# Attention keys cut into three chunks of 128 and one shared tail chunk; scores of batches 1 to 3 as stacked products

## The chip, the cores and the metric

The kernel runs on one core of one Trainium2 chip. The profile names the engines PE (TensorE, the matrix engine), PEld (its loading of weights), DVE (VectorE), ACT (ScalarE), POOL (GpSimd) and SP (SyncE, which issues most DMAs). The metric is the device time of one execution in microseconds; several executions are timed and their median is given. One more execution is profiled.

## What is computed

Softcapped attention over 4 batches, 12 heads, 448 positions and head width 64, and behind it two feed-forward layers over all 1792 positions, all in float32:

```python
scores = (q @ k^T) / sqrt(64)
scores = cap * tanh(scores / cap)
attn = softmax(scores)
x = attn @ v                      # heads side by side: 1792 x 768
x = relu(x @ w_in)**2 @ w_out     # 768 -> 2048 -> 768
h = x @ w2_in
out = (h * sigmoid(1.702 * h)) @ w2_out
```

## The kernel before

**Precision.** Every float32 operand is split into a rounded part and a rest (hi and lo), both in the engine's fast float32 form, and a product is made of two or three such products that add up in PSUM: hi x hi, hi x lo, lo x hi. The split takes one instruction on ACT (the copy that rounds) and one on DVE (the subtraction).

**Attention, by pairs of heads.** The path that runs is `bounded_cap`; `any_cap` (lines 21 and on) stands behind a branch for large caps and isn't taken. There are 6 pairs in each of 4 batches. `load_pair` fetches Q and K of a pair so that head A takes partitions 0 to 63 and head B 64 to 127 once they are transposed (`transposed`: by PE in batch 0, by DVE in batches 1 to 3). `prep_k` and `prep_q` split them into `kk` and `qq`. The 448 keys are cut into 4 chunks of 112. For each chunk `scores` makes, for each head, three products with 64 rows of contraction (line 893): 6 products, the heads alternating between the upper and the lower 64 rows. The result has keys on 112 partitions and both heads' 448 queries behind each other, 896 columns. `tanhs` and `exps` go over it on ACT, `split_hi` (ACT, in batch 0 DVE for chunks 0 and 2) and `split_lo` (DVE) split it into `phi` and `plo`, and `pv` multiplies it with the split V: 4 products per chunk (line 961). The sums of the exponentials over the keys are made in batch 0 by PE, 4 products per chunk with a matrix that has one column of ones (`key_sum`, line 947); in batches 1 to 3 DVE first adds the four chunks (`add_keys`, line 928), and PE sums the total.

**Feed-forward.** Each batch has 68 units of work (`units`); `product` (line 1198) makes 18 or 15 full products of 128 x 128 x 448 in a unit, `ahead` prepares weights for later units (`rebias` and the `wh` of `split_w` on ACT, `join` and the `wl` of `split_w` on DVE), `finish` takes the results out. In the first batch the weights come in a packed 64-bit form and need `rebias` and `join`; the joined weights are kept in DRAM for the other batches.

**Order.** `PLAN` gives each step of a pair its place, `attn_sub` runs one step of time for all pairs under way, a pair begins every 8 steps, and the main loop at the end sets as many steps of the next batch's attention behind each unit as spread them over a batch's units. The framework's scheduler then orders each engine's queue by what it reckons can start, within the limits of the tiles' buffers: `hi` and `lo` have 3 each (pool `e_p`), `x32` has 7, the K and Q tiles have 2. Each engine works through its queue in order. POOL issues the stores of batches 0 to 2 and the constants' memsets; SP issues the loads.

Of the kernel before, what the change touches and what calls it, by code (L numbers as in the profile page):

```python
# [677 lines left out]
def bounded_cap(ctx, tc, q, k, v, cap, w1, w2, w3, w4, out):  # L678
# [14 lines left out]
    nc = tc.nc  # L693
# [6 lines left out]
    NCH = S // CP  # L700
# [5 lines left out]
    Q_V = nc.sync  # L706
    Q_OUT = nc.gpsimd
# [24 lines left out]
    X32B = 7  # L732
# [34 lines left out]

    spread = [const.tile([P, 2, D], F32R, name=f"spread{i}") for i in range(NP)]
    sums = const.tile([P, S], F32, name="sums")
    rcp = const.tile([P, 2, S], F32R, name="rcp")  # L770

    def emit_const():
# [11 lines left out]
        nc.gpsimd.memset(f32(one[:, P - 1 : P]), 1.0)  # L784
        nc.gpsimd.memset(f32(rcp), 0.0)
# [15 lines left out]

    def load_pair(b, p):
        if b in DVE_QK:

            qt = ld.tile([P, S // 32, 32], F32, tag="q", name="qt")
            kt = ld.tile([P, S // 32, 32], F32, tag="k", name="kt")
            for t, src in ((kt, k), (qt, q)):
                for j in range(4):
                    Q_LOAD.dma_start(
                        out=t[32 * j : 32 * j + 32],  # L810
                        in_=src[b, 2 * p + j // 2, :, 32 * (j % 2) : 32 * (j % 2) + 32].rearrange(
                            "(c p) d -> p c d", p=32
                        ),
                    )
        else:
            qt = ld.tile([CP, NCH, 2, D], F32, tag="q", name="qt")
            kt = ld.tile([CP, NCH, 2, D], F32, tag="k", name="kt")
            for t, src in ((kt, k), (qt, q)):
                for j in range(2):
                    Q_LOAD.dma_start(  # L820
                        out=t[:, :, j, :], in_=src[b, 2 * p + j].rearrange("(p c) d -> p c d", c=NCH)
                    )
        raw[b, p] = (qt, kt)

    def transposed(b, t, name):

        if b in DVE_QK:
            y = ld.tile([P, S], F32, tag="tt", name=name)
            nc.vector.transpose(y, t.rearrange("p c d -> p (c d)"))
            return y  # L830
        ps = ps_x.tile([P, 512], F32, tag="x", name=name)
        for c in range(NCH):
            cols = slice(c, S, NCH) if name == "qps" else slice(c * CP, (c + 1) * CP)
            nc.tensor.transpose(ps[:, cols], t[:, c].rearrange("p h d -> p (h d)"), ident[:CP, :CP])
        return ps[:, :S]

    def load_v(b, p):
        vt = v_p.tile([CP, NCH, 2, D], F32, tag="vraw", name="vraw")
        for j in range(2):
            src = v[b, 2 * p + j]  # L840
            Q_V.dma_start(
                out=vt[:, :, j, :],
                in_=src.rearrange("(c p) d -> p c d" if b in DVE_QK else "(p c) d -> p c d", c=NCH),
            )
        vst[b, p] = vt

    def split_v(b, p, half):

        if half == 0:
            t = vst[b, p]  # L850
            vs = v_p.tile([CP, NCH, 4, D], F32R, tag="v", name="vs")
            vst[b, p] = (t, vs)
            nc.scalar.activation(vs[:, :, 0::3, :], t, AF.Copy)
        else:
            t, vs = vst[b, p]
            nc.vector.tensor_tensor(vs[:, :, 1:3, :], t, f32(vs[:, :, 0::3, :]), ALU.subtract)
            vst[b, p] = vs

    def prep_k(b, p, step):
# [60 lines left out]
    def add_keys(b, p, c):  # L920
# [3 lines left out]
        if c == 1:  # L924
            acc[b, p] = e_p.tile([CP, 2, S], F32, tag="acc", name="acc", bufs=1)
            et[b, p, NCH] = acc[b, p]
        a = acc[b, p]
        nc.vector.tensor_tensor(a, et[b, p, 0] if c == 1 else a, et[b, p, c], ALU.add)

    def key_sum(b, p, c):  # L930
# [5 lines left out]
        last = (p == p1 - 1 or not whole) and (c == NCH - 1 or not whole)  # L936
# [6 lines left out]
        hi, lo = hl[b, p, c]  # L943
        for j in range(2):
# [423 lines left out]
```

## Time and profile before

| | us |
|---|---|
| median of 3 timed runs | 1208.27 (1207.53 to 1212.91) |
| profiled execution | 1207.45 |
| its span in the profile | 1205.6 |

| engine | busy us | share of the span | instructions |
|---|---|---|---|
| PE | 1179.2 | 98% | 5832 |
| PEld | 1019.6 | 85% | 5832 |
| DVE | 848.8 | 70% | 1173 |
| ACT | 783.1 | 65% | 1129 |
| POOL | 48.4 | 4% | 83 |

The chain that ended last, followed back from the last instruction, is PE for 88% of the span, ACT for 7% and DVE for 2%. Of the 5832 matrix instructions 4608 belong to the feed-forward, 576 to the scores, 384 to the value products. A row of the timeline gives the start of an instruction, or of several alike in a row, how long they lasted from the first start to the last end, and what they read and write; matrix instructions overlap, so their price is read from one start to the next.

### The profile page before, as it was taken

The numbers are of one execution on the slowest core, as the hardware profiler recorded it, in microseconds if no ns is written. First come the engines' busy times: TensorE is split into PE (matmuls) and PEld (weight loads), VectorE is DVE, ScalarE is ACT, GpSimd is POOL, SyncE is SP. The second block draws the span as 40 slices with busy tenths as digits, with TensorE's granted clock in tenths as the row PEclk, the third lists the DMA queues.
The fourth block names the chain that finished last, engine by engine and source line by source line (L and its number), as shares of the span: only waits on it lengthen the run. The fifth ranks groups of instructions, "written<-read, shape, count | busy, mean of one in ns | idle before, by whom it ended". The sixth has DMA issues, their size and how long they took to land.

```text
span 1205.6 us, 15747 instructions
## 1 busy us (share of the span) xinstructions
PE 1179.2 (98%) x5832; PEld 1019.6 (85%) x5832; DVE 848.8 (70%) x1173; ACT 783.1 (65%) x1129; POOL 48.4 (4%) x83
## 2 busy tenths in 40 slices
PE   6999999999999999999999999999999999999996
PEld 4667988888777888888888888888899999999996
DVE  5799778998899956777577965667646753565354
ACT  6997898999878756677666566566643444344431
POOL 1000000000000400000000310000000310000000
PEclk9999999999999999999999999999999999999999
DMA  7555988788877855334323532223223442333333
GB/s 177 133 125 149 345 257 248 214 244 236 255 224 209 247 144 114 100 110 118 100 81 105 141 110 92 78 89 105 79 92 99 145 131 92 113 111 108 101 106 49
DMA packets 193225, 174.06 MB, mean 144 GB/s; under 512 B 116466, under 2 KB 165618, under 8 KB 193138
## 3 DMA queue, kind: packets, MB, share of 16 engines
q1 hardware_dynamic: 185266, 168.13, 46.9%
q0 software_dynamic: 2304, 4.13, 1.7%
q10 hardware_dynamic: 5568, 0.69, 0.4%
q8 instruction: 48, 0.79, 0.3%
q14 instruction: 39, 0.32, 0.1%
HBM read 142.25 MB, written 30.67 MB: 143 GB/s over the span
## 4 chain that ended last, share of the span: by engine, by line
PE 88%; ACT 7%; DVE 2%; issue 1%; SPq 1%; DMA 1%; DVEq 0%; ACTq 0%
PE mps L1198 76%; PE sps L893 5%; PE vps L961 5%; ACT e L904 2%; PE sums L947 1%; ACT e L900 1%; ACT phi L914 1%; ACT ct L979 1%; ACT wh L1178 1%; PE rps L1034 1%; ACT sx L1154 1%; SPq L820 0%; DVE plo L918 0%; DVE wl L1179 0%; DVE y L1161 0%
## 5 line engine op out<-in xcount | busy, mean ns | idle before, releaser
L1198 PE MATMUL mps<-g,wh 128*128 128x448 f32 x1536 | 442.2, 368 | 1.5 <-ACT g L1227 0.8
L1198 PE MATMUL mps<-xt,wh 128*128 128x448 f32 x1536 | 440.9, 368 | 0.5 <-ACT wh L1178 0.4
L1178 ACT ACTIVATE wh<-wraw 128x768 fp32r<-128x768 f32 (+1 forms) x204 | 164.7, 808 | 277.8 <-PE mps L1198 264.8
L1198 PEld LDWEIGHTS mps<-g,wh 128*128 128x128 f32 x1536 | 285.7, 188 | 36.9 <-ACT wh L1178 4.9
L1198 PEld LDWEIGHTS mps<-xt,wh 128*128 128x128 f32 x1536 | 286.0, 188 | 33.9 <-issue 5.1
L1179 DVE TENSOR_TENSOR wl<-wraw,wh 128x768 fp32r<-128x768 f32 (+1 forms) x204 | 185.4, 909 | 174.6 <-ACT wh L1178 173.0
L1198 PE MATMUL mps<-g,wl 128*128 128x448 f32 x768 | 281.3, 366 | 1.0 <-DVE wl L1179 1.0
L1198 PE MATMUL mps<-xt,wl 128*128 128x448 f32 x768 | 281.1, 366 | 0.3
L1198 PEld LDWEIGHTS mps<-g,wl 128*128 128x128 f32 x768 | 144.2, 188 | 14.2 <-DVE wl L1179 1.9
L1198 PEld LDWEIGHTS mps<-xt,wl 128*128 128x128 f32 x768 | 144.3, 188 | 13.3 <-DVE wl L1179 1.0
L1227 ACT ACTIVATE g<-r 128x448 fp32r<-128x448 f32 x128 | 73.4, 574 | 66.9 <-DVE r L1223 33.5
L918 DVE TENSOR_TENSOR plo<-e,phi 112x896 fp32r<-112x896 f32 x96 | 103.7, 1081 | 13.6 <-ACT phi L914 13.1
L1228 DVE TENSOR_TENSOR g<-r,g 128x448 fp32r<-128x448 f32 x128 | 79.6, 622 | 47.2 <-ACT g L1227 46.8
L904 ACT ACTIVATE e<-e,ecap 112x896 f32<-112x896 f32 x96 | 99.7, 1041 | 1.3
L893 PE MATMUL sps<-qq,kk 64*112 64x448 f32 x576 | 92.5, 404 | 2.7 <-ACT qq L879 1.7
L1240 DVE SCALAR_TENSOR_TENSOR y<-mps,y 128x448 f32<-128x448 f32 x96 | 59.5, 620 | 49.2 <-PE mps L1198 48.5
L900 ACT ACTIVATE e<-sps 112x896 f32<-112x896 f32 x96 | 87.2, 911 | 6.1 <-PE sps L893 5.9
L1256 POOL DMA_DIRECT2D out_dram<-o x72 | 45.2, 635 | 927.8 <-DVE o L1254 927.0
L914 ACT ACTIVATE phi<-e 112x896 fp32r<-112x896 f32 x84 | 79.6, 947 | 3.0 <-PE vps L961 1.2
L893 PEld LDWEIGHTS sps<-qq,kk 64*112 64x112 f32 x576 | 45.9, 174 | 40.3 <-issue 18.7
L961 PE MATMUL vps<-plo,vs 112*128 112x448 f32 x192 | 69.6, 374 | 3.4 <-DVE plo L918 3.4
L1179 DVE TENSOR_TENSOR wl<-y,wh 128x768 fp32r<-128x768 f32 (+1 forms) x68 | 61.5, 904 | 14.7 <-ACT wh L1178 14.2
(69 smaller groups left out, 1033.5 us busy)
## 6 DMA issues: line engine op xcount, KB each, us to landing
wraw<-keep SPq DMA_DIRECT2D x66, 768.0 KB, 4.3
wraw<-in_moe_w_in_dram SPq DMA_DIRECT2D x32, 766.5 KB, 6.5
wraw<-keep SPq DMA_DIRECT2D x36, 640.0 KB, 4.4
keep<-y SPq DMA_DIRECT2D x44, 384.0 KB, 3.2
wraw<-in_moe_w_out_dram SPq DMA_DIRECT2D x24, 638.8 KB, 6.1
wraw<-in_moe_w_out_dram SPq DMA_DIRECT2D x12, 766.5 KB, 6.6
keep<-y SPq DMA_DIRECT2D x24, 320.0 KB, 3.2
vraw<-in_v_dram SPq DMA_DIRECT2D x48, 112.0 KB, 3.8
```

What stands on the lines that cost most here:

```text
L893: nc.tensor.matmul(ps[:CP, j, :S], kk[r, ik, c * CP : (c + 1) * CP], qq[r, iq, :], start=(i == 0), stop=(i == 2),)
L900: nc.scalar.activation(e, sc.pop((b, p, c))[:CP, :, :S], AF.Tanh)
L904: nc.scalar.activation(e, e, AF.Exp, scale=ecap[:CP])
L914: nc.scalar.activation(hi, e, AF.Copy)
L918: nc.vector.tensor_tensor(lo, et[b, p, c], f32(hi), ALU.subtract)
L961: nc.tensor.matmul(pvp[b, p][j][:, :S], a, t[:, j, :], start=(c == 0 and n == 0), stop=(c == NCH - 1 and n == 1),)
L1178: nc.scalar.activation(hi[:, :kn], t[:, :kn], AF.Copy)
L1179: nc.vector.tensor_tensor(lo[:, :kn], t[:, :kn], f32(hi[:, :kn]), ALU.subtract)
L1198: nc.tensor.matmul(ps[:, :S], a[:, kk, :], r, start=(kk == 0 and i == 0), stop=(kk == kn - 1 and i == 2),)
L1227: nc.scalar.activation(g[:, 0, :], r, AF.Copy)
L1228: nc.vector.tensor_tensor(g[:, 1, :], r, f32(g[:, 0, :]), ALU.subtract)
L1240: nc.vector.scalar_tensor_tensor(y, ps[:, :S], scale, y, ALU.mult, ALU.add)
```

## The change

The 448 keys of a head become three full chunks of 128 and a tail of 64. The K tile is 512 columns wide with zeros in it, so that the tail of head A stands in columns 64 to 127 on its partitions and the tail of head B in columns 0 to 63 on its own; one tail chunk of 128 rows serves both heads, and its scores are 448 columns wide, not 896. V is loaded to match: head A's full chunks are its keys 64 to 447, head B's its keys 0 to 383, and one more slot holds both tails.

In batches 1 to 3 (`STACKED`) the hi and lo parts of Q lie above each other on the 128 partitions, in one tile per head, and K's hi and lo parts are each copied to the other 64 partitions by a DMA on POOL's queue (`prep_k`, step 3). One product of 128 rows then makes K hi with Q hi and with Q lo at once, a second one K lo with both: two products per head and chunk, four per chunk, and four for the tail. The splits of K and Q are done in two instructions of 64 partitions each. In batch 0 the three full chunks keep their six products of 64 rows; the tail has three of 128 rows.

`pv` has four products for a full chunk and four of 64 rows for the tail. `hi` and `lo` get two buffers instead of three, `x32` six instead of seven.

The diff, cut to its core:

```diff
-    NCH = S // CP
+    NCH = 4
+    TAIL = NCH - 1
+    KW = NCH * P
+    STACKED = (1, 2, 3)
...
+    Q_DUP = nc.gpsimd
...
-    X32B = 7
+    X32B = 6
...
+    kz = [const.tile([P, KW], F32, name=f"kz{i}") for i in range(2)]
...
+    def emit_zeros():
+        for t in kz:
+            nc.gpsimd.memset(t, 0.0)
...
     def load_pair(b, p):
+        kt = kz[p % 2]
...
-            kt = ld.tile([CP, NCH, 2, D], F32, tag="k", name="kt")
...
+            Q_LOAD.dma_start(out=kt[16:, :, 0, :], in_=ka)
+            Q_LOAD.dma_start(out=kt[32:, :, 1, :], in_=kb[:96])
+            Q_LOAD.dma_start(out=kt[:16, :, 1, :], in_=kb[96:])
+            Q_LOAD.dma_start(out=qt[:, :, 0, :], in_=qa)
+            Q_LOAD.dma_start(out=qt[:, :, 1, :], in_=qb)
...
     def load_v(b, p):
...
+        vt = v_p.tile([P, 2 * TAIL + 1, D], F32, tag="vraw", name="vraw")
+        va, vb = v[b, 2 * p], v[b, 2 * p + 1]
+        Q_V.dma_start(out=vt[:, 0 : 2 * TAIL : 2, :], in_=va[64:].rearrange("(c p) d -> p c d", p=P))
+        Q_V.dma_start(out=vt[:, 1 : 2 * TAIL : 2, :], in_=vb[: TAIL * P].rearrange("(c p) d -> p c d", p=P))
+        Q_V.dma_start(out=vt[64:, 2 * TAIL, :], in_=va[:64])
+        Q_V.dma_start(out=vt[:64, 2 * TAIL, :], in_=vb[TAIL * P :])
...
     def prep_k(b, p, step):
...
+            if stacked:
+                for j, r, o in halves():
+                    nc.scalar.activation(kk[r, j, 0, :], ps[r], AF.Copy)
+            else:
+                nc.scalar.activation(kk[:, 0, :], ps, AF.Copy)
...
+        elif stacked:
+            kk = prep[b, p][1]
+            for j, r, o in halves():
+                Q_DUP.dma_start(out=f32(kk[o, j]), in_=f32(kk[r, j]))
...
     def scores(b, p, c):
...
-        for i, (ik, iq) in enumerate(((0, 0), (0, 1), (1, 0))):
-            for j in range(2):
-                r = slice(64 * j, 64 * j + 64)
-                nc.tensor.matmul(
-                    ps[:CP, j, :S], kk[r, ik, c * CP : (c + 1) * CP], qq[r, iq, :],
-                    start=(i == 0), stop=(i == 2),
-                )
+        tail = c == TAIL
+        cols = slice(0, P) if tail else slice((c + 1) * P, (c + 2) * P)
+        if b in STACKED:
+            todo = [(0 if tail else j, kk[:, j, i, cols], qq[:, j, :]) for j in range(2) for i in range(2)]
+        elif tail:
+            todo = [(0, kk[:, ik, cols], qq[:, iq, :]) for ik, iq in ((0, 0), (0, 1), (1, 0))]
...
+    def width(c):
+
+        return slice(0, 1 if c == TAIL else 2)
...
-        hi = e_p.tile([CP, 2, S], F32R, tag="hi", name="phi")
-        lo = e_p.tile([CP, 2, S], F32R, tag="lo", name="plo")
+        hi = e_p.tile([P, 2, S], F32R, tag="hi", name="phi", bufs=2)[:, width(c), :]
+        lo = e_p.tile([P, 2, S], F32R, tag="lo", name="plo", bufs=2)[:, width(c), :]
...
+        if c == TAIL:
+            for j, r, o in halves():
+                nc.vector.tensor_tensor(a[o, j, :], a[o, j, :], e[o, 0, :], ALU.add)
...
+        if c == TAIL:
+
+            todo = [(j, vt[o, 2 * TAIL], t[o, 0, :]) for t in hl[b, p, c] for j, r, o in halves()]
...
-        -5: [(prep_q, 0)],
+        -5: [(prep_q, 0), (prep_k, 3)],
```

**PE's order, at unit 34 of batch 0's feed-forward** (about 230 us in the trace of before). Units are counted from 0. Names: `mps` is a unit's product, `vps` a value product, `sps` scores, `sums` the key sums, each with its buffer number; `wh` and `wl` are split weights. Before, from the end of unit 33 to the start of unit 34:

```order
L1198 MATMUL mps_2443<-g_2210,wh_2378 128x448 x2
L1198 MATMUL mps_2443<-g_2210,wl_2379 128x448
L961 MATMUL vps_2244<-phi_2388,vs_2087 128x448
L961 MATMUL vps_2244<-plo_2389,vs_2087 128x448
L961 MATMUL vps_2245<-phi_2388,vs_2087 128x448
L961 MATMUL vps_2245<-plo_2389,vs_2087 128x448
L1198 MATMUL mps_2489<-xt_675,wh_2418 128x448 x2
L1198 MATMUL mps_2489<-xt_675,wl_2419 128x448
```

The changed kernel at the same place: the end of unit 33, the tail's four products, the next scores.

```order
L1282 MATMUL mps_2452<-g_2218,wh_2384 128x448 x2
L1282 MATMUL mps_2452<-g_2218,wl_2385 128x448
L1045 MATMUL vps_2252<-phi_2394,vs_2093 128x448
L1045 MATMUL vps_2253<-phi_2394,vs_2093 128x448
L1045 MATMUL vps_2252<-plo_2395,vs_2093 128x448
L1045 MATMUL vps_2253<-plo_2395,vs_2093 128x448
L967 MATMUL sps_2538<-qq_2209,kk_2055 128x448 x4
L1030 MATMUL sums_2578<-phi_2478,one_118 128x448
```

And after seven more products the end of that block and the start of unit 34:

```order
L1045 MATMUL vps_2584<-plo_2487,vs_2434 128x448
L967 MATMUL sps_2601<-qq_2209,kk_2055 128x448 x4
L1045 MATMUL vps_2584<-phi_2589,vs_2434 128x448
L967 MATMUL sps_2699<-qq_2543,kk_2399 128x448
L1045 MATMUL vps_2583<-plo_2590,vs_2434 128x448
L1045 MATMUL vps_2584<-plo_2590,vs_2434 128x448
L967 MATMUL sps_2699<-qq_2543,kk_2399 128x448 x3
L1045 MATMUL vps_2583<-phi_2645,vs_2434 128x448
L1045 MATMUL vps_2584<-phi_2645,vs_2434 128x448
L1282 MATMUL mps_2500<-xt_675,wh_2425 128x448 x2
```

Before, the four products of one chunk stand between units 33 and 34. Now 30 products stand there: the tail, the last scores and the sums of one pair, and the value products of two chunks and part of a third of the next pair.

**ACT's order at the same place.** `wh` 2378, 2418 and 2463 are the weights of units 33, 34 and 35; `e` is tanh (from `sps`) or exp, `phi` the rounding copy. Before:

```order
L1178 ACTIVATE wh_2378<-y32_2333 128x640
L1245 ACTIVATE xt_703<-y_1294 128x448
L900 ACTIVATE e_2391<-sps_2346 112x896
L904 ACTIVATE e_2391<-e_2391,ecap_113 112x896
L914 ACTIVATE phi_2477<-e_2391 112x896
L1245 ACTIVATE xt_913<-y_1294 128x448
L1178 ACTIVATE wh_2418<-y32_2374 128x768
L1154 ACTIVATE sx1_116<-wraw_2341 128x768
L900 ACTIVATE e_2480<-sps_2429 112x896
L1178 ACTIVATE wh_2463<-y32_2414 128x768
```

The changed kernel, where `wh_2384` (nine rows further up) are the weights of unit 33 and `wh_2425` those of unit 34:

```order
L982 ACTIVATE e_2489<-e_2489,ecap_113 128x896
L992 ACTIVATE phi_2486<-e_2397 128x896
L1329 ACTIVATE xt_1018<-y_1296 128x448
L1063 ACTIVATE ct_2530<-vps_2252 64x448
L1063 ACTIVATE ct_2530<-vps_2253 64x448
L992 ACTIVATE phi_2589<-e_2489 128x896
L978 ACTIVATE e_2592<-sps_2538 128x896
L982 ACTIVATE e_2592<-e_2592,ecap_113 128x896
L992 ACTIVATE phi_2645<-e_2592 128x896
L1262 ACTIVATE wh_2425<-y32_2380 128x768
L1238 ACTIVATE sx1_116<-wraw_2349 128x768
```

Before, five instructions stand between the weights of unit 33 and those of unit 34, one of them a `phi`. Now there are seventeen, and these are the last of them: three of the `phi` read or replace what the block on PE works on.

**SP's order at the start of the program** (its first loads; `kz` and `kt` are K tiles, `capt` the cap). Before:

```order
L820 DMA kt<-in_k_dram 112x4x64 x2
L820 DMA qt<-in_q_dram 112x4x64 x2
L773 DMA capt<-in_cap_dram 128x1
L820 DMA kt<-in_k_dram 112x4x64 x2
L820 DMA qt<-in_q_dram 112x4x64 x2
L841 DMA vraw<-in_v_dram 112x4x64 x3
```

The changed kernel, from the same place; three more rows for the first pair's V follow the last one shown:

```order
L850 DMA qt<-in_q_dram 112x4x64
L847 DMA kz_120<-in_k_dram 112x4x64
L848 DMA kz_120<-in_k_dram 96x4x64
L849 DMA kz_120<-in_k_dram 16x4x64
L851 DMA qt<-in_q_dram 112x4x64
L786 DMA capt<-in_cap_dram 128x1
L847 DMA kz_121<-in_k_dram 112x4x64
L848 DMA kz_121<-in_k_dram 96x4x64
L849 DMA kz_121<-in_k_dram 16x4x64
L850 DMA qt<-in_q_dram 112x4x64
L851 DMA qt<-in_q_dram 112x4x64
L871 DMA vraw<-in_v_dram 128x3x64
```

Q's first half has moved ahead of K, K takes three DMAs instead of two, and V's first tile takes four instead of two, which stand behind two more.

## Rows read from the trace of the kernel before

**Rows 1.** Busy time by stretch: us, PE, PEld, DVE, ACT, POOL, clock, DMA
```profile
36.00:94.50 58.50, 54.46 (x265) 36.32 (x264) 52.15 (x73) 56.82 (x78) 0.00 (x0) 1.00 0.46 114
94.50:408.50 314.00, 311.07 (x1527) 260.51 (x1528) 274.50 (x367) 272.05 (x385) 8.35 (x14) 1.00 0.81 244
184.00:348.00 164.00, 162.20 (x811) 135.59 (x811) 144.36 (x191) 145.48 (x203) 0.00 (x0) 1.00 0.79 229
408.50:690.00 281.50, 281.19 (x1406) 246.98 (x1405) 206.52 (x287) 179.72 (x262) 15.75 (x26) 1.00 0.43 115
690.00:962.30 272.30, 272.12 (x1357) 242.34 (x1356) 175.72 (x243) 155.32 (x227) 13.85 (x23) 1.00 0.32 99
```
**Rows 2.** Waits, total us, times, longest: 94.5 to 408.5, then 408.5 to 962.3
```profile
ACT wh L1178 <- PE mps L1198: 9.4, 9, 1.7
...
ACT wh L1178 <- PE mps L1198: 174.8, 119, 3.2
```
**Rows 3.** Timeline of ACT (start, us, instruction), first and last of nine
```profile
238.42 0.85 ACT L1178 ACTIVATE wh<-y 128x768 fp32r<-128x768 f32 x1
...
244.38 0.54 ACT L979 ACTIVATE ct<-vps 64x448 f32<-64x448 f32 x1
```
**Rows 4.** Timeline of PE: full products, a run of six, a run of two
```profile
902.76 0.36 PE L1198 MATMUL mps<-xt,wl 128*128 128x448 f32 x1
...
904.79 0.56 PE L1198 MATMUL mps<-xt,wh 128*128 128x448 f32 x2
...
485.09 0.36 PE L1198 MATMUL mps<-g,wl 128*128 128x448 f32 x1
485.39 0.86 PE L893 MATMUL sps<-qq,kk 64*112 64x448 f32 x6
486.18 0.67 PE L1198 MATMUL mps<-g,wh 128*128 128x448 f32 x2
...
329.76 0.37 PE L1198 MATMUL mps<-xt,wl 128*128 128x448 f32 x1
...
330.45 0.47 PE L1198 MATMUL mps<-g,wh 128*128 128x448 f32 x1
```
**Rows 5.** Groups of ACT: count, busy us, mean ns of one, idle before
```profile
L904 ACT ACTIVATE e<-e,ecap 112x896 f32<-112x896 f32 x96 | 99.7, 1041 | 1.3
L900 ACT ACTIVATE e<-sps 112x896 f32<-112x896 f32 x96 | 87.2, 911 | 6.1 <-PE sps L893 5.9
L914 ACT ACTIVATE phi<-e 112x896 fp32r<-112x896 f32 x84 | 79.6, 947 | 3.0 <-PE vps L961 1.2 <-PE sums L947 0.5
L1227 ACT ACTIVATE g<-r 128x448 fp32r<-128x448 f32 x128 | 73.4, 574 | 66.9 <-DVE r L1223 33.5 <-DVE r L1219 32.9
L1222 ACT ACTIVATE r<-mps 128x448 f32<-128x448 f32 x64 | 33.8, 528 | 4.8 <-PE mps L1198 4.8
L879 ACT ACTIVATE qq<-qps,qs 128x448 fp32r<-128x448 f32 x24 | 15.6, 649 | 0.1
```
**Rows 6.** Groups of DVE, columns as in rows 5
```profile
L918 DVE TENSOR_TENSOR plo<-e,phi 112x896 fp32r<-112x896 f32 x96 | 103.7, 1081 | 13.6 <-ACT phi L914 13.1
L981 DVE TENSOR_TENSOR x<-vps,ct 64x448 f32<-64x448 f32 x48 | 29.7, 618 | 1.4 <-ACT ct L979 0.7
L882 DVE SCALAR_TENSOR_TENSOR qq<-qps,qs,qq 128x448 fp32r<-128x448 f32 x24 | 16.3, 678 | 1.4 <-ACT qq L879 1.3
L870 DVE TENSOR_TENSOR kk<-kps,kk 128x448 fp32r<-128x448 f32 x24 | 14.8, 616 | 4.5 <-ACT kk L867 4.5
```
**Rows 7.** Timeline of the start: SP's issues of V, ACT's first V, a memset
```profile
7.20 1.95 SPq L841 DMA_DIRECT2D vraw<-in_v_dram  x3
...
10.58 0.63 ACT L853 ACTIVATE vs<-vraw 112x512 fp32r<-112x512 f32 x1 [4.22 <-DMA vraw<-in_v_dram]
...
0.88 0.74 POOL L776 MEMSET sx<- 128x768 int32 x1
```
**Rows 8.** DMA issues of POOL: count, KB each, median us to landing
```profile
out_dram<-o POOLq DMA_DIRECT2D x72, 56.0 KB, 2.9
```

More of the change, by code (lines that the diff above doesn't have):

```diff
@@ L766, in bounded_cap @@
     one = const.tile([P, 2 * P], F32R, name="one")
+    two = const.tile([P, 2 * P], F32R, name="two")
+    kz = [const.tile([P, KW], F32, name=f"kz{i}") for i in range(2)]
     spread = [const.tile([P, 2, D], F32R, name=f"spread{i}") for i in range(NP)]
@@ L784, in emit_const @@
         nc.gpsimd.memset(f32(one[:, P - 1 : P]), 1.0)
+        nc.gpsimd.memset(f32(two), 0.0)
+        nc.gpsimd.memset(f32(two[64:, P - 1 : P]), 1.0)
+        nc.gpsimd.memset(f32(two[:64, P : P + 1]), 1.0)
         nc.gpsimd.memset(f32(rcp), 0.0)
@@ L815, in load_pair @@
         else:
+            kt = kt.rearrange("p (c h d) -> p c h d", h=2, d=D)
             qt = ld.tile([CP, NCH, 2, D], F32, tag="q", name="qt")
[L817 to L822 removed]
+            ka, kb, qa, qb = (
+                src[b, 2 * p + j].rearrange("(p c) d -> p c d", c=NCH) for src in (k, q) for j in range(2)
+            )
@@ L832, in transposed @@
         for c in range(NCH):
-            cols = slice(c, S, NCH) if name == "qps" else slice(c * CP, (c + 1) * CP)
-            nc.tensor.transpose(ps[:, cols], t[:, c].rearrange("p h d -> p (h d)"), ident[:CP, :CP])
-        return ps[:, :S]
+            nc.tensor.transpose(
+                ps[:, c:n:NCH], t[:, c].rearrange("p h d -> p (h d)"), ident[: n // NCH, : n // NCH]
+            )
+        return ps[:, :n]
     def load_v(b, p):
[L838 to L844, printed above, removed]
+        vt = v_p.tile([P, 2 * TAIL + 1, D], F32, tag="vraw", name="vraw")
[4 more added lines that the diff above has]
+        Q_V.dma_start(out=vt[:64, 2 * TAIL, :], in_=vb[TAIL * P :])
         vst[b, p] = vt
@@ L924, in add_keys @@
         if c == 1:
-            acc[b, p] = e_p.tile([CP, 2, S], F32, tag="acc", name="acc", bufs=1)
+            acc[b, p] = e_p.tile([P, 2, S], F32, tag="acc", name="acc", bufs=1)
             et[b, p, NCH] = acc[b, p]
-        a = acc[b, p]
-        nc.vector.tensor_tensor(a, et[b, p, 0] if c == 1 else a, et[b, p, c], ALU.add)
+        a, e = acc[b, p], et[b, p, c]
+        if c == TAIL:
+            for j, r, o in halves():
+                nc.vector.tensor_tensor(a[o, j, :], a[o, j, :], e[o, 0, :], ALU.add)
+        else:
+            nc.vector.tensor_tensor(a, et[b, p, 0] if c == 1 else a, e, ALU.add)
     def key_sum(b, p, c):
@@ L935, in key_sum @@
         first = (p == p0 or not whole) and (c == 0 or not whole)
-        last = (p == p1 - 1 or not whole) and (c == NCH - 1 or not whole)
+        last = (p == p1 - 1 or not whole) and (c == TAIL or not whole)
         if first:
@@ L942, in key_sum @@
         ps = sps[g] if whole else sps[g][:, 0]
-        hi, lo = hl[b, p, c]
-        for j in range(2):
-            w = one[:CP, P - 1 - row - j : 2 * P - 1 - row - j]
-            for n, t in enumerate((hi, lo)):
-                nc.tensor.matmul(
-                    ps[:, :S], w, t[:, j, :],
-                    start=first and j == 0 and n == 0, stop=last and j == 1 and n == 1,
-                )
+        todo = []
+        for j in range(1 if c == TAIL else 2):
+            w = (two if c == TAIL else one)[:, P - 1 - row - j : 2 * P - 1 - row - j]
+            todo += [(w, t[:, j, :]) for t in hl[b, p, c]]
+        for n, (w, t) in enumerate(todo):
+            nc.tensor.matmul(
+                ps[:, :S], w, t, start=first and n == 0, stop=last and n == len(todo) - 1,
+            )
     def pv(b, p, c):
```

96 lines of the change are left out of this document (65 added, 31 removed).

## The prediction, before the result was known

> **What bounds the kernel now.** The busy times of the stretches come first [rows 1]. I cut the span where the feed-forward of a batch begins, by counting 1152 products a batch: a head of 94.5 us (attention of batch 0), then F0 (314.0 us), F1 (281.5), F2 (272.3) and F3. Between F0's products runs the attention of batch 1, between F1's that of batch 2, between F2's that of batch 3. TensorE is busy 311.1, 281.2 and 272.1 us of F0 to F2, at the full granted clock of 1.00 (the 2.4 GHz level), so its instructions set the time from 94.5 us on. In the head it is ACT: busy 56.8 of 58.5 us from 36 us on, with VectorE (DVE) close behind at 52.2.
>
> F0 is not like F1 and F2. In the waits of the stretches [rows 2] ACT is held up by TensorE (`wh` behind `mps`) for 174.8 us in F1 and F2 together, but for 9.4 us in F0: there ACT has next to no lead. From 184 to 348 us it works 145.5 and DVE 144.4 of 164 us [rows 1]. Instructions of ACT that follow each other overlap in part: the nine from 238.42 to 244.92 have durations of 7.1 us and fill 6.5, a factor of 0.92 [rows 3]. So a busy share of 0.9 is nearly full. All TensorE instructions of F0, costed as below, come to 303 us; it takes 314, so 11 us are already lost to late inputs, against 3 in F1 and 2 in F2.
>
> **The change part by part.**
>
> Price of a product: ten full ones start from 902.76 to 904.79, 0.203 each. The six 64-row products of a chunk: 1.09 us from the start of the full one before them (485.09) to the next full one (486.18), less 0.203, is 0.887. A run of two: 0.69 from 329.76 to 330.45, less 0.203, is 0.485 [rows 4]. So a pair of narrow ones side by side costs about 0.20, and going into the narrow form and out of it another 0.28. Four narrow ones are then 0.69, between the runs of two and of six.
>
> Scores of batches 1 to 3: four full products are 0.812 instead of 0.887, 0.075 less; 18 pairs of heads x 4 chunks = 72 times: -5.4 us. The same rows weighed against a rule: the Trainium skill, "TensorEngine Tiling (Array Packing)", section Theoretical Speedup, grants a contraction of at most 64 rows up to twice the speed; by that six narrow products would cost three full ones, 0.61, the stacked form would add 0.20 a chunk, and the sum would stand near 1223 us. The same page's Key Properties say that a change of mode drains the engine, which fits the 0.28.
>
> Value products of batches 1 to 3: 12 full ones as before and a tail of four narrow ones, 0.69 instead of 0.812, 18 times: -2.2. Broken runs: the old order has the 204 narrow score products of F0 in 44 runs where sixes would make 34: 10 x 0.28 = -2.8; eight of these runs are of odd length: -0.8. The new order splits four more tails in two: +1.1. Sum on TensorE after the head: **-10 us**. It doesn't fall where one expects it: the new order draws about 0.9 of a pair from F1 into F0, so that TensorE's sums go from 303 to 303, 279 to 270 and 271 to 269. F1 and F2 have lead to spare, so I count the 10 in full (bounds -8 and -11).
>
> ACT and DVE, per pair. A tail of 448 columns instead of 896: tanh 0.911 to 0.528 (as the tanh `r`), phi 0.947 to 0.57 (as the copy `g`), exp 1.041 to 0.60 by the same proportion; K's copy has 64 columns more, V's 64 less: -1.2 us of ACT [rows 5]. DVE: lo 1.081 to 0.62, K +0.07: -0.4 [rows 6]. For batch 0's six pairs that is ACT -7.2, DVE -2.4. In batches 1 to 3 a half of 64 partitions costs what the whole does (64x448 add 0.618, 128x448 0.616 [rows 6]), so two in place of one add on ACT some 0.65 for K and 0.65 for Q, which eats the 1.2. On DVE: K +0.75, Q +0.68, K's transpose +0.09, the last key sum as two halves +0.15, lo -0.46, V -0.07: +1.1 a pair, 6.8 us in F0. Both engines also get the 0.9 pair that is drawn forward, some 14 us each.
>
> Head. The gain lies between DVE's 2.4 and ACT's 7.2; ACT is nearer to full, so -5. Against it stands the start of SP's queue: three issues take 1.95 us, ACT's first `vs` waits for V until 10.58, and the `qq` for the first scores stands behind it on ACT [rows 7]. Before V's first tile is whole now come four more issues (one for each of the first two K, two for V), 0.6 each: +2.4. Head: **-2.6** (bounds -7 and 0). What TensorE saves in the head, some 0.8 us a pair, lies beside ACT. The zeroing of the K tiles on POOL (a memset of 768 columns takes 0.74 [rows 7], each K tile has 512) is hidden behind Q's load, which now goes first; without that cover it would cost 0.5.
>
> F0. `hi` and `lo` get two buffers instead of three: a split on ACT then waits for the value products of the chunk two before it, not three. The order shows what follows. At five places of F0 (behind units 33, 40, 47, 54, 61, counted from 0) much of a pair stands in one block between two units, and ACT's splits there wait for TensorE while ACT still owes the weights of the next unit. At unit 34 ACT works from `phi_2486`, which waits for the tail's products, to `wh_2425`: 0.95 + 0.57 + 2 x 0.54 + 0.95 + 0.91 + 1.04 + 0.95 + 0.85 = 7.3 [rows 3, 5], times 0.92 is 6.7, behind a tail of 0.69: 7.4 us. TensorE has 26 products and the tail for that time, 6.0 us. So 1.4 us are lost if ACT is on time. It need not be: between `wh_2384` and `phi_2486` stand nine more instructions, 6.8 us, beside unit 33 with 15 x 0.203 = 3.05; up to 3.7 more. That is 1.4 to 5.1 a place, 7 to 26 for five. I take 3.2, 16 in all, since ACT is seldom early in F0 [rows 2], and 3 elsewhere: 19 instead of 11, +8 (bounds -4 and +18).
>
> K's copies to the other 64 partitions are 36 DMAs on POOL, in pairs; its stores land after 2.9 us [rows 8], so a pair of copies takes between 2.9 and twice that, some 4. The order puts four units or more, 13 us, between K's split and the first score, but for two pairs: the first of batch 1 (two units) and the one whose first scores stand inside the block at unit 34. I count 1 us for these two (bounds 0 and 8). 20 copies stand ahead of POOL's first 24 stores, so none that F0 needs queues behind a store. F0: **+9 us**. SP's four more issues a pair are some 2.5 us in 45, beside other work. Six `x32` instead of seven hold up the first `x` of the next batch until F0's last splits: nothing, as F1 has lead; without it, one such step of 0.6.
>
> Sum against the profiled execution (1207.45 us, 1205.6 of it span; the median shown is 0.8 above): -2.6 + 9 - 10 = -3.6, about **1203.5 us**.
>
> **Rivals.**
> - The cover holds: ACT is early at the five places. F0 then loses 8 to 11 us, as now (-3 to 0), and the head gives 4: 1190.5 to 1193.5. For it: TensorE is idle only 2.9 us of F0 [rows 1]. Against: a lead of 9.4 against 174.8 us of waiting.
> - Slower, by the blocks of F0: each costs 5.1, five 25.5, with 3 elsewhere 28.5 instead of 11, +17.5; so late an ACT eats the head's gain too: +17.5 - 10 gives 1215. It turns the sum from 24 us lost in F0 on, 4.2 a place. For it: ACT and DVE get more work in just this stretch. Against: between the blocks F0 gets lighter.
> - The stacked form is dearer, as by the rule above: 0.20 more a chunk instead of 0.075 less, 72 times, +19.8 on the forecast: 1223. Rows 4 speak against it.
> - K's copies come late: one pair in three uncovered, 6 x 4.2 = 25: 1228. For it: this wait is new on TensorE's own path; against: the 13 us.
>
> **How the numbers follow.** Forecast 0.46, cover holds 0.24, blocks 0.22, dearer stacking 0.03, late copies 0.05. The forecast's own range is 1198 to 1210. For 8 in 10 I go to 1192, inside the cover's span, and to 1216, just past the blocks. A measurement of this kernel tells about 0.5%, 6 us, from no change. Below 1202.2 lie the cover and two fifths of the forecast: 0.42. Within 6 us the rest of the forecast and a little of the blocks: 0.30. Above 1214.3 most of the blocks and the last two: 0.28.
>
> **What would show it.** Right: stacked scores at 0.81 a chunk, value tails near 0.69; F1 near 273 us and F2 near 270; F0 near 323, with TensorE idle or slow at five places behind `phi` or `wh`; the first `qq` near 13.5; the head near 92. Wrong: F0 under 314 (cover) or above 330 (blocks), `sps` waiting for a DMA, or four full scores dearer than 0.89.

## The result, and the profile after

The changed kernel takes 1222.41 us (median of 4, 1220.56 to 1226.79) against 1208.33 (1207.53 to 1212.91) for the kernel before on the same chip: a ratio of 1.0114, interval 1.0077 to 1.0151. It is 1.1% slower, and above my range, which ended at 1216. The profiled execution took 1220.56 us, 13.1 more than that of before.

Busy time of F0, F1 and F2 in the changed kernel, to be read beside [rows 1] (stretch, its length, then PE, PEld, DVE, ACT, POOL with their instructions, granted clock, DMA share, GB/s):

```profile
93.50:435.30 341.80, 322.98 (x1489) 280.50 (x1490) 299.16 (x408) 287.51 (x417) 19.35 (x35) 0.96 0.80 238
435.30:705.80 270.50, 270.40 (x1332) 246.88 (x1331) 199.30 (x283) 171.37 (x260) 18.78 (x32) 1.00 0.49 129
705.80:975.50 269.70, 269.61 (x1326) 245.71 (x1325) 182.53 (x259) 153.95 (x233) 18.48 (x31) 1.00 0.34 106
```

The head is 1.0 us shorter, F1 11.0, F2 2.6, the last stage the same. F0 alone is longer, by 27.8 us, and its granted clock is 0.96 where before it was 1.00.

F0 and F1 are best read together, since the new order draws attention from F1 into F0: F0 to F2 come to 882.0 us against 867.8, 14.1 longer.

Where in F0? I list the starts of matrix instructions that follow the one before them by more than 0.33 us, and take 0.204, the normal distance, from each: the **late starts**. Before they come to 7.2 us in F0, now to 35.7. Of these, 29.1 lie at the five places of the prediction: 3.0 at unit 34, 6.3 at 41, 6.1 at 48, 7.1 at 55, 6.6 at 62. PE's longest waits in F0 (total us, times, longest):

```profile
PE mps L1282 <- ACT wh L1262: 3.1, 4, 1.9
PE sums L1030 <- ACT e L978: 2.2, 1, 2.2
PE rps L1118 <- DVE x L1126: 2.2, 1, 2.2
PE vps L1045 <- DVE x L1065: 2.2, 1, 2.2
PE sps L967 <- ACT e L978: 2.1, 1, 2.1
PE sums L1030 <- ACT phi L992: 2.0, 1, 2.0
```

The `x` are DVE's: the wait at unit 34 is for `x` L1065, which takes a value product out of PSUM, and one of the two at unit 55 for `x` L1126. The others are for ACT: `wh` at 41, `e` at 48 and 55, `phi` at 62. The place at unit 48 on PE's timeline (start, length, what it does, in brackets the idle time and its releaser):

```profile
325.28 0.47 PE L967 MATMUL sps<-qq,kk 128*128 128x448 f32 x1
327.96 0.54 PE L1030 MATMUL sums<-phi,one 128*128 128x448 f32 x1 [2.22 <-ACT e L978]
...
329.96 1.12 PE L1282 MATMUL mps<-xt,wh 128*128 128x448 f32 x2 [0.33 <-ACT wh L1262]
...
332.24 0.57 PE L1282 MATMUL mps<-xt,wl 128*128 128x448 f32 x1
...
334.85 0.66 PE L1282 MATMUL mps<-xt,wh 128*128 128x448 f32 x2
335.35 0.36 PE L1282 MATMUL mps<-xt,wl 128*128 128x448 f32 x1
```

and ACT, the engine waited for here:

```profile
318.91 0.54 ACT L1306 ACTIVATE r<-mps 128x448 f32<-128x448 f32 x1 [3.11 <-PE mps L1282]
319.51 0.95 ACT L992 ACTIVATE phi<-e 128x896 fp32r<-128x896 f32 x1
...
327.02 0.89 ACT L978 ACTIVATE e<-sps 128x896 f32<-128x896 f32 x1
327.94 1.10 ACT L1063 ACTIVATE ct<-vps 64x448 f32<-64x448 f32 x2
329.06 0.84 ACT L1262 ACTIVATE wh<-y 128x768 fp32r<-128x768 f32 x1
```

ACT waits 3.11 us for a product and then works without a break through attention, from 318.91 to 329.06, before it reaches the weights of the next unit. PE runs dry for 2.22 us, then again for 0.33. And then seven products, from 332.24 to 334.85, start 0.373 us apart, against 0.203 in [rows 4]. The granted clock in these stretches:

```profile
328.20:334.80 6.60, 6.27 (x16) 4.68 (x16) 6.32 (x9) 6.50 (x10) 0.00 (x0) 0.50 0.91 272
334.90:345.00 10.10, 10.10 (x51) 9.38 (x50) 9.15 (x14) 8.50 (x13) 0.00 (x0) 0.99 0.62 202
366.00:372.00 6.00, 3.63 (x9) 2.32 (x9) 5.90 (x10) 5.89 (x8) 0.00 (x0) 0.50 0.75 226
407.00:413.00 6.00, 5.27 (x14) 4.20 (x14) 5.64 (x9) 5.93 (x9) 0.28 (x1) 0.50 0.87 209
```

Behind the gaps at units 48, 55 and 62 it is 0.50, the 1.2 GHz level, and the products behind the gaps start at half pace. Gaps of over 0.45 us from start to start make 25.6 us of F0's late starts, those between 0.33 and 0.45 make 10.1, of which 7.8 lie where the clock is low.

### The profile page after: what moved, and what is told of

Same layout as the page of the kernel before. It is cut to its first block, busy times and chain, and to the rows that moved or that the text cites. A ratio compares the mean times of both kernels' runs of the same rounds, so it can differ in the third digit from the quotient of the medians.

```text
span 1218.8 us, 15803 instructions
## 1 busy us (share of the span) xinstructions
PE 1170.5 (96%) x5658; PEld 1039.2 (85%) x5658; DVE 871.3 (71%) x1227; ACT 783.4 (64%) x1165; POOL 69.6 (6%) x126
## 4 chain that ended last, share of the span: by engine, by line
PE 82%; ACT 7%; DVE 6%; issue 2%; DMA 1%; SPq 1%; POOL 0%; DVEq 0%; ACTq 0%; POOLq 0%
PE mps L1282 72%; PE sps L967 5%; PE vps L1045 4%; PE sums L1030 1%; ACT e L982 1%; DVE plo L996 1%; ACT phi L992 1%; ACT wh L1262 1%; DMA vraw<-in_v_dram 1%; ACT e L978 1%; ACT sx L1238 1%; ACT ct L1063 1%; DVE sums L1103 1%; PE rps L1118 1%; DVE wl L1263 0%
## 5 line engine op out<-in xcount | busy, mean ns | idle before, releaser
L1282 PEld LDWEIGHTS mps<-g,wh 128*128 128x128 f32 x1536 | 290.0, 190 | 33.4 <-ACT wh L1262 4.9
L1282 PEld LDWEIGHTS mps<-xt,wh 128*128 128x128 f32 x1536 | 289.3, 189 | 28.6 <-ACT wh L1262 1.6
L1282 PEld LDWEIGHTS mps<-g,wl 128*128 128x128 f32 x768 | 145.5, 189 | 16.3 <-DVE wl L1263 4.4
L967 PE MATMUL sps<-qq,kk 128*128 128x448 f32 (+1 forms) x414 | 98.1, 387 | 7.2 <-ACT qq L932 2.8
L996 DVE TENSOR_TENSOR plo<-e,phi 128x896 fp32r<-128x896 f32 x96 | 91.9, 962 | 5.5 <-ACT phi L992 4.6
L982 ACT ACTIVATE e<-e,ecap 128x896 f32<-128x896 f32 x96 | 90.5, 946 | 1.3
L967 PEld LDWEIGHTS sps<-qq,kk 128*128 128x128 f32 (+1 forms) x414 | 67.8, 194 | 21.0 <-issue 3.7
L978 ACT ACTIVATE e<-sps 128x896 f32<-128x896 f32 x96 | 78.1, 816 | 8.9 <-PE sps L967 5.9
L992 ACT ACTIVATE phi<-e 128x896 fp32r<-128x896 f32 x84 | 69.7, 838 | 4.1 <-PE vps L1045 2.0
L1238 ACT ACTIVATE sx<-wraw 128x768 f16<-128x768 bf16 (+1 forms) x68 | 69.6, 1024 | 0.5 <-DVE y L1245 0.3
L1262 ACT ACTIVATE wh<-y 128x768 fp32r<-128x768 f32 (+1 forms) x68 | 54.5, 802 | 21.6 <-DVE y L1245 12.7
```

The source lines that it names most:

```text
L967: nc.tensor.matmul(ps[:, u, :S], x, y, start=all(t[0] != u for t in todo[:n]), stop=all(t[0] != u for t in todo[n + 1 :]),)
L978: nc.scalar.activation(e, sc.pop((b, p, c))[:, width(c), :S], AF.Tanh)
L982: nc.scalar.activation(e, e, AF.Exp, scale=ecap)
L992: nc.scalar.activation(hi, e, AF.Copy)
L996: nc.vector.tensor_tensor(lo, et[b, p, c], f32(hi), ALU.subtract)
L1238: nc.scalar.activation(z, words(n, BF16)[:, :, :, 2], AF.Copy)
```

## The experiments

Three theories of what makes F0 longer. **A**: `hi` and `lo` with two buffers hold ACT up, as the prediction had it. **B**: the stacked form's halved splits and K's copies load ACT, DVE and POOL. **C**: SP's queue has 14 loads per pair in batches 1 to 3 instead of 10, and the scheduler, which lays out all queues by its own reckoning, places the attention later and bunched, in blocks. A block is 20 or more attention products of PE between two units; the order of before has two in F0 (29 and 27 products), the changed one five (30, 37, 36, 29, 33), three of them behind 52 to 108 products of the feed-forward without a break.

All runs; stretches and waits come from one profile each, times and ratios from all executions. A ratio is against executions of the kernel before on the same chip as the run, so it isn't the quotient of two medians of the table; that kernel's median was 1208.9 beside e1, e3, e6 and e7, 1208.3 beside e8 to e11, 1211.5 beside e12 to e14 and 1208.0 beside e15. The sum F0 to F2 is the fair length, since orders move attention between the stages.

| kernel | median us | ratio, 95% | blocks | F0 | F0 to F2 | late starts in F0 | ACT waits for weight loads in F0 |
|---|---|---|---|---|---|---|---|
| before | 1208.3 | | 2 | 314.0 | 867.8 | 7.2 | 0.4 |
| changed | 1222.4 | 1.0114 (1.0077 to 1.0151) | 5 | 341.8 | 882.0 | 35.7 | 0.2 |
| e1: before, two buffers | 1209.4 | 1.0005 (0.998 to 1.003) | 2 | 313.2 | 868.0 | 9.0 | 0.6 |
| e10: before, more loads | 1220.7 | 1.0108 (1.0088 to 1.0127) | 3 | 323.3 | 873.0 | 13.6 | 0.3 |
| e3: changed, three buffers, no stacked form | 1217.6 | 1.0053 (1.0026 to 1.0079) | 5 | 334.2 | 878.9 | 27.2 | 0 |
| e8: e3 with V on POOL | 1202.0 | 0.9949 (0.9925 to 0.9972) | 0 | 303.2 | 856.7 | 6.3 | 1.5 |
| e15: e8 with the first pair's V on SP | 1205.4 | 0.9971 (0.9952 to 0.999) | 2 | 312.7 | 866.6 | 16.2 | 1.6 |
| e9: changed, three buffers, V on POOL | 1220.9 | 1.0096 (1.0075 to 1.0117) | 2 | 317.3 | 868.4 | 20.8 | 9.6 |
| e11: before, V on POOL | 1213.9 | 1.0050 (1.0032 to 1.0069) | 0 | 310.4 | 868.8 | 11.3 | 6.4 |
| e6: changed, kept weights stored by POOL | 1221.5 | 1.0085 (1.0053 to 1.0117) | 0 | 332.2 | 882.5 | 35.4 | 38.8 |
| e7: changed, Q, K and V on POOL | 1231.3 | 1.0172 (1.0116 to 1.0227) | 0 | 331.6 | 883.0 | 36.4 | 36.2 |
| e12: changed, Q of batches 1 to 3 on POOL | 1210.9 | 0.9992 (0.9965 to 1.0018) | 0 | 321.6 | 871.1 | 24.7 | 26.4 |
| e13: e12, batch 1 not stacked | 1207.3 | 0.9966 (0.9945 to 0.9986) | 0 | 316.2 | 866.5 | 19.8 | 29.8 |
| e14: e12, nothing stacked, three buffers | 1206.1 | 0.9955 (0.9931 to 0.9979) | 0 | 310.3 | 865.3 | 14.5 | 18.8 |

### Buffers alone: theory A

```diff
-        hi = e_p.tile([CP, 2, S], F32R, tag="hi", name="phi")
-        lo = e_p.tile([CP, 2, S], F32R, tag="lo", name="plo")
+        hi = e_p.tile([CP, 2, S], F32R, tag="hi", name="phi", bufs=2)
+        lo = e_p.tile([CP, 2, S], F32R, tag="lo", name="plo", bufs=2)
```

> The kernel before with one edit: hi and lo get two buffers instead of three. Theory A (the two buffers make F0 long, as I predicted for the blocks, only larger): F0 goes from 314 us to between 330 and 342, the granted clock falls to the 1.2 GHz level behind long gaps as it does in the changed kernel, and the time is 1222 to 1236 us. Theory B (stacking's halved splits and K copies load ACT and DVE): nothing of that is here, 1208 to 1210 us. Theory C (the four more loads of a pair on SP's queue make the scheduler bunch the attention into five blocks): the loads are the old ones, and this kernel's order has two long blocks in F0 (28 and 31 attention products between two units) as before has (29 and 27), so F0 stays under 318 us and the time under 1213.

F0 is 313.2 us and the ratio 1.0005: with two buffers instead of three and nothing else changed, F0 doesn't grow. The changed kernel's own trace agrees: the wait that A rests on, of ACT's rounding copy `phi` for value products, comes to 2.0 us in all of F0 (total, times, longest).

```profile
ACT phi L992 <- PE vps L1045: 2.0, 3, 0.7
```

A falls as a cause by itself.

### Loads alone: theory C

In the kernel before, the same bytes in more loads (K's in the same way):

```diff
+            x = src.rearrange("(c p) d -> p c d" if b in DVE_QK else "(p c) d -> p c d", c=NCH)
+            for c in ((0, 2), (2, 4)) if b in DVE_QK else ((0, 4),):
+                Q_V.dma_start(out=vt[:, c[0] : c[1], j, :], in_=x[:, c[0] : c[1], :])
```

> The kernel before with one edit: in batches 1 to 3 each of V's two loads and of K's last two is cut in two, so that SP has four more loads per pair, with the same bytes and all arithmetic unchanged. The order now has three blocks in F0, of 36, 43 and 44 attention products (before: two, 29 and 27). Theory C: F0 goes from 314 us to between 324 and 334, with gaps at units 48, 55 and 62 and falls of the clock behind them; the time is 1214 to 1224. Theories A and B, and any that puts the loss down to the arithmetic: F0 stays at 312 to 316 us and the time at 1206 to 1211.

The median is 1220.7 us, 1.0108: by the time as much as the change loses, with not one arithmetic instruction altered. The one profile, of the shortest of its four executions (1216.0), shows less, and F0 falls just short of C's range: it is 9.3 us longer, F1 4.4 shorter, since the order draws attention forward, and F0 to F2 are 5.1 longer, where the change has 14.1. Late starts go from 7.2 to 13.6. At the three blocks they are 1.2, 3.2 and 3.5 where before had 0.9, 0.9 and 1.8, and the clock falls behind one of the three (0.50 from 395.0 to 398.4 us). Another 3.0 us lie in the last stage, 2.4 of them in products that start 0.207 us apart instead of 0.203 from its middle on; the profiles of e1, e14 and e15 have these too, so they aren't the loads' doing. So more loads alone do lengthen F0, by a third of what the change does; where the rest of this run's median comes from, no trace shows.

### The changed kernel's loads without its arithmetic

```diff
-    STACKED = (1, 2, 3)
+    STACKED = ()
...
+        hi = e_p.tile([P, 2, S], F32R, tag="hi", name="phi")[:, width(c), :]
+        lo = e_p.tile([P, 2, S], F32R, tag="lo", name="plo")[:, width(c), :]
```

> The changed kernel without its stacked form (all batches take the 64-row products; no halves, no copies of K) and with three buffers for hi and lo. The loads on SP's queue are those of the changed kernel, and its order still has five blocks in F0 (23, 47, 35, 37 and 29 attention products between two units). Theories A and B: two suspected causes are gone, F0 comes back to 312 to 318 us, and the time is 1196 to 1203 us. Theory C: the blocks are still there, so F0 keeps gaps at units 34, 41, 48, 55 and 62 with falls of the clock behind them; F0 is 328 to 340 us and the time 1213 to 1224.

With three buffers and no stacked form F0 is still 334.2 us, inside C's range. Next, the same kernel with V's loads on POOL, which takes the blocks out of the order and leaves arithmetic, buffers and bytes as they are:

```diff
-    Q_V = nc.sync
+    Q_V = nc.gpsimd
```

> As the kernel with three buffers and no stacked form, and with the loads of V issued by POOL instead of SP. Work, buffers and bytes are the same; the order has no block of 20 or more attention products in F0 (that kernel had five, and F0 was 334.2 us). Theory C (the blocks in the order cause the gaps): F0 is 308 to 318 us, no fall of the clock at units 34 to 62, and the time 1193 to 1202. If the bare load on ACT and DVE were the cause, F0 stays at 328 to 338 and the time at 1212 to 1222. Theory D, out of the run with the keep stores on POOL: without the blocks ACT comes early to the weights and waits for their DMA (38.8 us there, with the products' results r, g and y queued behind it on ACT); then F0 is 322 to 335 too, but with PE behind r, g and y, not behind wh and e.

F0 falls by 31.0 us to 303.2, below the range, and F0 to F2 by 22.2; late starts go from 27.2 to 6.3, and the clock is at 1.00:

```profile
98.00:401.20 303.20, 299.02 (x1483) 257.52 (x1484) 266.98 (x367) 257.50 (x379) 28.55 (x44) 1.00 0.82 250
```

This is the fastest version, 0.9949; e13, e14 and e15 also lie below 1 with their whole intervals. Its head is 98.0 us instead of 94.2, for which its timeline of ACT has the row:

```profile
16.75 1.06 ACT L1238 ACTIVATE sx<-wraw 128x768 f16<-128x768 bf16 x1 [8.90 <-DMA wraw<-in_moe_w_in_dram]
17.68 0.61 ACT L932 ACTIVATE qq<-qps,qs 128x448 fp32r<-128x448 f32 x1
```

With V gone from SP the order puts a weight's rebias ahead of the first `qq`, and ACT waits 8.90 us for its load. So I gave the first pair's V back to SP:

```diff
     def load_v(b, p):
+        Q_V = nc.gpsimd if b or p >= 1 else nc.sync
```

> As the kernel with three buffers, no stacked form and V's loads on POOL (1202 us; head 98.0, F0 303.2), but V of the very first pair is loaded by SP again. In the other kernel ACT's order puts the first weights' rebias ahead of the first qq and waits 8.9 us for their load; here the first qq stands behind V as in the changed kernel. The order has two small blocks in F0, 25 and 24 attention products at units 55 and 62. Theory C: the head is 93 to 95 us, F0 305 to 313 with the gaps at these two places alone, and the time 1198 to 1204. If blocks had nothing to do with it, F0 would stay at 303.

The head is 93.4 us, but two blocks are back in the order and F0 is 312.7: as expected, though the time came out 1.4 above the range. The gaps aren't at the two blocks alone, as C had it: of 16.2 us of late starts 5.3 lie there, 5.3 at the beginning of F0 (102 to 110 us, with the clock at 0.50 from 104.0 on) and 3.9 around 220 us. So the blocks went and came with the queue of V's loads, and F0 with them, but in this run the blocks make only about a third of the 9.9 us of late starts that it has over e8.

### Other loads moved: a second way to lose

The changed kernel with the stores of joined weights on POOL (`Q_KEEP = nc.gpsimd`), with all of Q, K and V on POOL, and with Q's loads of batches 1 to 3 there:

> The changed kernel with one edit: the stores that keep the joined weights are issued by POOL instead of SP, so that SP's queue holds the loads alone. Two buffers, stacked form, halves and K copies stay; the copies now share POOL's queue with the stores. Its order has no block of 20 or more attention products in F0. Theory C: the gaps at units 34, 41, 48, 55 and 62 go, and with them the falls of the clock; F0 is 312 to 320 us and the time 1192 to 1201. Theories A and B: buffers and extra work are as in the changed kernel, F0 stays at 335 to 345 us and the time at 1216 to 1226. If K's copies come late behind the stores, the stacked scores wait for a DMA, at about 4 us a pair for up to six pairs.

> The changed kernel with one edit: the loads of Q, K and V are issued by POOL, so that SP's queue holds the weight loads and the keep stores alone. The order has no block of 20 or more attention products in F0. Theory C: as with the stores moved, F0 is 312 to 320 us; the head may lose some us, because POOL issues more slowly than SP at the start, or gain, because two queues issue at once: 1192 to 1204. Theories A and B: 1216 to 1226. If this kernel is fast and the one with the stores moved is not (or the reverse), the place on SP's queue matters, not the crowding.

> The changed kernel with one edit: Q's four loads of a pair are issued by POOL in batches 1 to 3 (batch 0 is left as it is). Stacked form, halves, K copies and two buffers stay. The order has no block of 20 or more attention products in F0. Theory C alone: F0 comes down from 341.8 us to between 298 and 312 (less attention is drawn into F0 than in the changed kernel, so F1 grows to about 280), and the time is 1190 to 1200. Theory B (with the blocks gone, the stacked form's halves and K copies still cost): F0 is 318 to 330 and the time 1207 to 1220, with the stacked scores or ACT behind K's copies, which wait on POOL's queue behind loads of Q whose tile isn't free.

None has a block, yet F0 is 332.2, 331.6 and 321.6 us, and all three times lie above C's ranges. C as I had it was wrong here: without blocks F0 need not be short. The third lies inside the ranges that I gave for B, but neither PE nor ACT waits in its F0 for K's copies. In the waits of these runs something stands that the changed kernel has next to nothing of (0.2 us): ACT's rebias `sx` waiting for the load of weights, 38.8, 36.2 and 26.4 us. In the run with Q's loads on POOL, at unit 49, first ACT, then PE in a fence of its own:

```profile
319.38 1.04 ACT L982 ACTIVATE e<-e,ecap 128x896 f32<-128x896 f32 x1
324.68 0.92 ACT L1238 ACTIVATE sx<-wraw 128x640 f16<-128x640 bf16 x1 [4.25 <-DMA wraw<-in_moe_w_out_dram]
325.46 0.51 ACT L1306 ACTIVATE r<-mps 128x448 f32<-128x448 f32 x1
```

```profile
326.68 1.12 PE L1282 MATMUL mps<-xt,wh 128*128 128x448 f32 x2 [3.35 <-DVE r L1307]
327.60 0.58 PE L1282 MATMUL mps<-xt,wl 128*128 128x448 f32 x1
```

ACT stands 4.25 us before weights that haven't landed, the `r` that PE needs stands behind them in its queue, PE is idle 3.35 us and the next products start at half clock. That is theory D. The two kinds of loss differ in what PE mostly waits for: `wh`, `e`, `phi` and `x` behind blocks, `r`, `g` and `y` behind late weights. The waits for weights don't count one for one: from e12 to e13 they grow from 26.4 to 29.8 us while the late starts shrink from 24.7 to 19.8. Why these orders have the rebias so early isn't settled. With all loads on POOL the head also grew to 104.9 us. From the run with Q's loads on POOL I took the stacked form of batch 1 away, and then the rest of it, with three buffers for `hi` and `lo`:

> As the one before, with the stacked form in batches 2 and 3 alone: batch 1, whose attention runs beside F0, takes the 64-row products, without halves and K copies, still with two buffers. No block in the order. If the time is that of the one before within 4 us, stacking costs nothing once the blocks are gone (theory C alone). If it is 10 to 20 us below it, with F0 at 300 to 308, stacking has a price of its own in F0 (theory B), through K's copies on POOL or the halves on DVE. Expected by theory C: 1192 to 1200.

> As the one before, without the stacked form in any batch and with three buffers for hi and lo. No block in the order. Beside the one before it tells what the third buffer is worth in F0 once the blocks are gone: theory A gives it 3 us or more of F0; theory C none. Against the kernel with V's loads on POOL (1202 us, F0 303.2, head 98.0), batch 0 keeps its loads on SP, so the head is 93 to 95 us again and the time 1194 to 1200.

Both came out above their ranges, 1207.3 against 1192 to 1200 and 1206.1 against 1194 to 1200. From e12 to e13, F0 to F2 fall by 4.6 us and the medians by 3.6: that is B's share, a few us and not 10 to 20. The third buffer and the last stacking together change F0 to F2 by 1.2 more, and the medians (1207.3 and 1206.1) can't be told apart: F0 gains 5.9, F1 and F2 lose 4.7 without the cheaper scores.

### Two more

The changed kernel with three buffers, V on POOL and less of other buffers; and the kernel before with V on POOL:

> The changed kernel, stacked form and all, with three buffers for hi and lo (paid for with two buffers of e instead of three, one transposed K or Q and one output tile) and the loads of V on POOL. Its order has two blocks in F0, 23 and 20 attention products, where the changed kernel has five of 29 to 37. Theory C: F0 is 312 to 322 us and the time 1192 to 1202, ahead of both kernels. Theory D (late weights) or K's copies late behind V's loads on POOL: F0 is 325 to 338 us and the time 1208 to 1222.

> The kernel before with the loads of V issued by POOL; its order has no block of 20 or more attention products in F0 (before: two). Theory C: F0 falls from 314 us to between 306 and 312, the time is 1199 to 1206. Theory D (late weights): F0 rises to between 318 and 330. If neither the blocks nor the loads matter, F0 stays at 313 to 315 us and the time at 1206 to 1211.

The first has F0 at 317.3 us, as C had it, but its time is 1220.9: the head is 99.4 and the last stage 252.4 instead of 243, where DVE waits 7.8 us for the output's stores, which have one tile instead of two. The second shows F0 at 310.4 but F0 to F2 unchanged (868.8), and a head of 100.0 with the same early rebias as above (a wait of 8.06 us at 14.46). So V on POOL is no gain by itself.

## Why the prediction was wrong

**Right.** TensorE's prices: four stacked products take 0.80 us from start to start, value tails 0.90 less the 0.204 of the product ahead, 0.70 (predicted 0.81 and 0.69):

```profile
501.16 0.36 PE L1282 MATMUL mps<-xt,wl 128*128 128x448 f32 x1
501.45 0.47 PE L1045 MATMUL vps<-phi,vs 64*128 64x448 f32 x2
501.76 0.37 PE L1045 MATMUL vps<-plo,vs 64*128 64x448 f32 x2
502.06 0.47 PE L1282 MATMUL mps<-g,wh 128*128 128x448 f32 x1
...
603.74 0.97 PE L967 MATMUL sps<-qq,kk 128*128 128x448 f32 x4
604.54 0.37 PE L1282 MATMUL mps<-g,wh 128*128 128x448 f32 x1
```

So the rival of 0.03, the dearer stacked form, falls: in [rows 4] six narrow products cost 0.887 us, as much as 4.4 full ones and not three. F1 came to 270.5 and F2 to 269.7 (predicted 273 and 270), 13.6 less than before where I counted 10. K's copies land after 4.2 us, as estimated, and no instruction of F0 waits for one; the rival with late copies falls. The first `qq` starts at 12.82 (13.5), the head is 93.5 (92). The first `qq` is 1.7 us later than before, not 2.4, so the queue cost less than I had, and ACT's gain in the head is nearer 2.7 than 5. ACT's waits for `mps` in F0 are 8.6 us beside the 9.4 of [rows 2]: it has no more lead than before.

**Wrong: the price of the five places, and what makes them.** I had them in the order, at the right units, behind `phi` or `wh`, and took 3.2 us each, 16, with bounds of 1.4 to 5.1. They cost 29.1, 5.8 each. With that term F0 was to grow by 9 us; it grew by 27.8, and this is where the sum fails: head -1.0, F0 +27.8, F1 and F2 -13.6 make the 13.1 us, where I had -2.6, +9 and -10. (My -3.6 from 1207.45 is 1203.9, not 1203.5; nothing hangs on it.) The step went wrong in three points.

1. The bound had no clock in it. [rows 1] show 1.00 for all of F0, and I priced what follows a gap at 0.203. Of the 29.1 us, gaps over 0.45 make 21.8, 4.4 a place, still inside my bounds; smaller distances, most of them at half clock, make the other 7.3. Where the clock falls, a gap is paid again behind it.
2. I chose the middle, 3.2, "since ACT is seldom early in F0". The same rows spoke for the upper end: an engine that works 145.5 of 164 us is late wherever its work is bunched. The argument that F0 gets lighter between the blocks didn't help: there ACT waits, as the 3.11 us at 318.91 show. And I reckoned with ACT alone: at units 34 and 55 PE waits 2.2 us each for DVE's `x`.
3. I put the loss at the blocks down to `hi` and `lo` having two buffers, with splits that wait for value products. In all of F0 that wait comes to 2.0 us. What the runs show in its place is SP's loads: with two buffers alone F0 stays as it was; with four more loads alone it grows; with the loads and three buffers it stays long; with V's loads off SP it is short. The prediction counted the four loads a pair as 2.5 us "beside other work". As a wait that holds: no instruction of F0 waits for a load of Q, K or V in the changed kernel. But the order of all engines is laid out ahead of the run, and there the loads count.

The rival "blocks" had the right places, at 5.1 each, and gave 1215, though by the same two buffers. What it lacks is the clock, and 6.6 us of late starts outside the places, where I had 3; the 11 us that I took as lost before are 7.2 by the starts.

**Not settled.** How the scheduler reckons a load isn't seen in any trace; shown is that orders and F0 change when nothing but loads does. That just the four added loads make the five blocks isn't shown: four added to the kernel before make three, and no run has the changed kernel with ten loads per pair on SP. Of the 27.8 us in F0, e3 leaves 20.2 with neither stacking nor two buffers; how the other 7.6 split between those two in the bunched order wasn't tried.

## What to carry to other kernels

When a scheduler lays out the queues, an edit to the number of DMAs on one queue is an edit to the order on every engine: look for long runs of one kind of work in the new order and price those first. Where an engine is busy for nine tenths, take the upper price for a block that it must work through, and add what the clock takes behind the gap. If arithmetic gains come with more loads, try other queues for them in the same step and look at the new order: here V's loads on POOL turned 1217.6 into 1202.0 us, while other moves (e6, e7) lost as much as the blocks. Merging the loads wasn't tried.

## What the runs showed of the hardware

- The granted clock fell to 0.50 behind idle gaps on TensorE within F0, where PE was busy for 323.0 of 341.8 us: behind the gap that ended at 327.96 it is 0.50 in 328.2 to 334.8, with PE busy for 6.27 of these 6.60 us, and 0.99 from 334.9 on. It did not fall behind every gap: one of 2.5 us from start to start that ended at 243.71 left it at 1.00 in this row of the changed kernel:

```profile
240.00:252.00 12.00, 9.52 (x44) 7.60 (x43) 11.84 (x16) 11.05 (x15) 0.00 (x0) 1.00 0.59 165
```

- The store of joined weights, 384 KB, landed after 3.7 us (median) from SP's queue in the changed kernel and after 6.2 from POOL's in e6:

```profile
keep<-y POOLq DMA_DIRECT2D x44, 384.0 KB, 6.2
```

- Executions of one kernel spread more than I had counted on: e12's ten lie between 1205.1 and 1217.4 us. One profile then misleads by some us, above all about the head: e1's was 100.5 us, before's 94.5, and only the buffers of `hi` and `lo` differ. The traces show where: from 16 to 25 us PE starts 28 instructions in e1 and 45 before, and toward the end of the head e1 has a stretch at half clock, first row, that the kernel before, second row, has not:

```profile
93.30:100.00 6.70, 6.38 (x16) 5.16 (x17) 4.88 (x7) 3.52 (x7) 0.00 (x0) 0.50 0.00 0
93.30:100.00 6.70, 6.65 (x33) 5.82 (x32) 6.43 (x10) 3.19 (x5) 0.00 (x0) 1.00 0.28 84
```
